# First MLP round of a fused attention, gating and MLP kernel: raw loads queued two slots later, written tiles kept six slots, a tenth tile, deferred VectorE halves, and other orders at the opening and the end

## The chip, the cores and the metric

The kernel runs on one core of a Trainium2 chip. The metric is the device time of one execution in microseconds (us), taken as the median of several runs. The engines are TensorE (PE), VectorE (DVE), ScalarE (ACT), GpSimd (POOL) and SyncE, whose DMA queue is SPq in the trace. Each works through its own instructions in the order in which they were written, and waits for the others on semaphores. All DMAs of this part of the program are issued by SyncE, in one queue.

## The reference

Everything is float32. Sigmoid attention over 4 x 12 heads of 448 rows feeds a gated MLP, and that feeds a channel MLP with a residual:

```python
h = np.maximum(x @ w_in, 0.0)                       # gated MLP
u, v = h[..., :512], h[..., 512:]
v_s = np.einsum('ts,bsd->btd', w_spatial, layernorm(v)) + b_spatial[None, :, None]
x = (u * v_s) @ w_out                               # (4, 448, 768)
xn = (x - mu) / np.sqrt(var + 1e-06) * g_ln         # channel MLP
ch = np.maximum(xn @ w_ch1, 0.0) @ w_ch2            # 768 -> 3072 -> 768
return x + ch
```

The kernel splits each float32 operand into a high part (a cast) and a low part (x minus the cast), and takes each product as three matmuls: high by high, high by low, low by high. The weights arrive as 64-bit floats, which the kernel decodes to float32 with shifts and scalings.

## The kernel before

The program has four stages. Up to some 249 us it computes attention, with the projections of the gated MLP and some weight decoding beside it. From 249 to 284 us it ends the gated MLP's projections and begins the spatial product, and a generator `after_stream` decodes and splits one more set of weights beside them. The spatial product and the output projection last to some 372 us. Then comes the channel MLP, in two rounds of twelve cells: the first on 1024 rows (512 columns a product), from 372 to about 820 us, the second on 768 rows.

One cell takes one of twelve weight groups `g`. Its first product (`w_ch1`) has seven sub-products in Strassen's manner, the P steps, each accumulated in a PSUM bank of its own kind, X or Y; its second product has seven or eight S steps, into the banks `acc`. Steps of neighbouring cells alternate: P 0 of cell i, S 0 of cell i-1, P 1, S 1, and so on. Each step is nine matmuls and is one slot; a cell has fourteen slots, here called s=0 to s=13, with P k at s=2k and S k at s=2k+1 (an eighth S step is behind s=13). Between the steps other work is written out: `settle(t)` is called after each step and issues what `plan` has put at slot `t` of the table `later`, then gives the queued DRAM writes their turn (`tick`), then gives tiles back, then fetches weights.

What lies around the change:

- The evacuation of a P step: `copied` is an ACT copy (L1262), `summed` a DVE add from PSUM (L1266), an ACT relu (L1267) and an ACT cast to the high part (L1251); `low` is the DVE subtraction of the low part (L1257). A later P step that begins a new sum in the bank waits for that evacuation. S3 (the sixth P step, s=10) and A22 (the seventh, s=12) both use X; `add` (L1349) is the DVE addition of an S step's result.
- Weights of groups 2 to 10 (`LATE`) are decoded in the first round. `load` (L353) brings 768 KB of raw words, `scale` is two ACT instructions (L387, L392), `bits` one of DVE (L396). `make` (L807, POOL) forms a sum of two pieces, `split` is an ACT cast (L812) and a subtraction (L813, on POOL for `w_ch1` and on DVE for `w_ch2`) into a tile of 768 columns of `t_all`, and `put` queues the tile's write to DRAM (`wscr`, L902), for the second round.
- Four tiles a cell (T1, T3, T2, T4 of `w_ch2`, at s=6, 7, 8 and 9) are made only for the second round: `staged` writes them out and gives the tile back some slots later. All tiles come from the list `w_free`, first in, first out: eight tiles, and a ninth after the opening.
- A raw buffer's next load is planned in the slot of the `bits` that ends its use. SyncE's queue is in order, so a load that waits for `bits` holds what is behind it.

Of the kernel before, what the change touches and what calls it, by code (L numbers as in the profile page):

```python
# [18 lines left out]
P = 128  # L19
# [51 lines left out]
R_SIZE, T_SIZE, F_SIZE, Q_SIZE = 30976, 6400, 12288, 3072  # L71
# [16 lines left out]
PLACE_W_T = [768 * k for k in range(8)]  # L88
PLACE_OUT = [23552, 24320]
# [24 lines left out]
LAST = [SEVEN[k] for k in (0, 5, 1, 2, 3, 4, 6)]  # L114
# [20 lines left out]
AFTER_JOBS = "d0 d1 - e0 11 e1 21 =T1 22 =T3 T1 =T2 T3 =T4 T2 - T4"  # L135
# [144 lines left out]
def sigmoid_attention_gmlp_mlp(ctx: ExitStack, tc, q, k, v, w_in, w_sp, w_out, g_ln, w1, w2, out):  # L280
# [512 lines left out]
    class Weights:  # L793
# [104 lines left out]
    puts = []  # L898
    put_after = [5]

# [131 lines left out]
    put_after[0] = 1  # L1032

    def after_stream():
        outs = Ring(R, 0, 0)
        outs.blocks = [Block(R, o, 2 * HALF) for o in PLACE_OUT]
        for grp, m in AFTER:
# [4 lines left out]
            for job in AFTER_JOBS.split():  # L1042
                tick()
                weights[grp].do(m, job, outs, nc.scalar.copy)
                yield
        while puts:
# [122 lines left out]
    for j, (u, c) in enumerate(order):  # L1169
# [10 lines left out]
        if j > 11:  # L1180
            proj.turn_parked(order[j - 2][1], banks, nc.vector.tensor_copy)
# [8 lines left out]
        if j == 12:  # L1190
            xn_of(j)
# [6 lines left out]
    X, Y = (ps_1.tile([P, 512], F32, tag="ps1", name="ps1") for _ in range(2))  # L1198
# [3 lines left out]
    w_free = deque(Block(T, o, 2 * HALF) for o in PLACE_W_T)  # L1202
# [13 lines left out]
    class Hidden:  # L1216
# [19 lines left out]
        def product(self, x, name):  # L1236
            ps = acc[0][:, 0] if (self.i, x) == (0, "A12") else {"A12": Y, "S1": Y, "S4": Y}.get(x, X)
# [32 lines left out]
        def s_add(self, name):  # L1270
# [9 lines left out]
            nc.vector.tensor_tensor(self.rt(out), self.rt(a), self.rt(b), op=op)  # L1280
            self.r[name] = self.r.pop(out)
            if name in ("S3", "S4"):
                self.drop({"S3": "H11", "S4": "S2"}[name])
            self.high(name)

        def after(self, x, ps):
# [25 lines left out]
        def step(self, k):  # L1312
            steps = self.steps()
            if k == 0 and self.i and hidden[self.i - 1].seven:
# [3 lines left out]
            for j in range(3):  # L1318
                if self.two:
# [3 lines left out]
                    if (self.i, k) == (2 * NGRP - 1, 6):  # L1323
                        self.add(ps, out, slice(j, j + 1))
                        self.store(out, j)
# [8 lines left out]
            if (self.i, k) == (2 * NGRP - 1, 6):  # L1334
                return
            if out:
                self.add(ps, out)
            if self.i == 2 * NGRP - 1 and k in (1, 4, 5):
                for j in range(3):
                    self.store(steps[k][4], j)  # L1340
# [316 lines left out]
```

## Time and profile before

| | |
|---|---|
| device time, median of 3 runs | 1111.88 us (1111.39 to 1111.99) |
| device time of the profiled execution | 1110.46 us |
| its span in the trace | 1108.6 us |
| PE busy | 1025.7 us (93%) |
| DVE, ACT, POOL busy | 769.9, 502.4, 317.0 us |
| mean granted PE clock | 0.969 |
| DMA | 251.6 MB, mean 227 GB/s |

A busy PE is not PE at its peak: the granted clock tells how fast it runs while busy (1.00 is 2.4 GHz, 0.50 is 1.2 GHz). In the timeline rows a number in square brackets is the engine's idle time before that instruction, and what ended it. Of a busy time with a count behind it (x2), the row covers several instructions in a run.

### The profile page before, as it was taken

The page shows a single profiled execution, that of the slowest core. Times are in us where ns is not written, and L with a number is a line of the kernel's source. Part 1 is how long each engine was busy: PE and PEld are TensorE (multiplying, and loading weights), DVE is VectorE, ACT ScalarE, POOL GpSimd, SP SyncE. Part 2 cuts the span into 40 slices and gives each one's busy share as a digit, 9 for nine tenths or more (in the row PEclk, how much of TensorE's full clock was granted, in tenths as well). Part 3 has the DMA queues.
Part 4 walks back from the last instruction along what each step waited for, and adds up shares of the span by engine and source line. Part 5 has one row for each costly group of instructions (what it writes and reads, how often), then busy time and mean ns, then how long its engine had stood idle before and what let it go on. Part 6 is the DMA issues. An engine that isn't in the chain of part 4 may idle for free.

```text
span 1108.6 us, 14832 instructions
## 1 busy us (share of the span) xinstructions
PE 1025.7 (93%) x5221; PEld 852.6 (77%) x5221; DVE 769.9 (69%) x999; ACT 502.4 (45%) x823; POOL 317.0 (29%) x266
## 2 busy tenths in 40 slices
PE   9999999998999999977977977979799999999996
PEld 5557666687899878755855855858688999999995
DVE  4679888356848678755655646655787779777776
ACT  5765454454646444645445445444432333333331
POOL 3614133023127404634534534532610012000000
PEclk9999999998999999989988988989899999999999
DMA  8857888566224675685575575667599898888884
GB/s 248 264 186 246 294 257 302 185 202 233 83 100 140 215 275 182 219 280 171 181 274 171 191 265 174 207 246 238 183 308 325 252 333 249 249 248 250 249 250 155
DMA packets 95097, 251.59 MB, mean 227 GB/s; under 512 B 12720, under 2 KB 27056, under 8 KB 94896
## 3 DMA queue, kind: packets, MB, share of 16 engines
q1 hardware_dynamic: 89616, 237.23, 64.8%
q0 software_dynamic: 1760, 7.36, 2.1%
q10 hardware_dynamic: 3648, 6.06, 1.6%
q8 instruction: 42, 0.69, 0.3%
q14 instruction: 31, 0.25, 0.1%
HBM read 163.82 MB, written 86.78 MB: 226 GB/s over the span
## 4 chain that ended last, share of the span: by engine, by line
PE 66%; DMA 8%; DVE 8%; issue 7%; POOL 6%; ACT 5%; SPq 0%; POOLq 0%; DVEq 0%; ACTq 0%
PE ps L341 11%; PE ps L342 10%; PE ps L343 10%; DMA wscr<-t_all 7%; PE acc L341 7%; PE acc L342 7%; PE acc L343 7%; PE psa L551 5%; PE ps L511 4%; POOL f_all L807 3%; POOL t_all L813 2%; DVE f_all L1349 1%; PE ps L524 1%; DVE f_all L396 1%; ACT t_all L812 1%
## 5 line engine op out<-in xcount | busy, mean ns | idle before, releaser
L341 PE MATMUL ps<-r_all,t_all 128*128 128x384 f32 (+1 forms) x480 | 182.2, 380 | 61.3 <-DVE f_all L1266 59.5
L1349 DVE TENSOR_TENSOR f_all<-acc,f_all 128x1152 f32<-128x1152 f32 (+2 forms) x135 | 201.5, 1493 | 37.5 <-PE acc L343 37.4
L342 PE MATMUL ps<-r_all,t_all 128*128 128x384 f32 (+1 forms) x480 | 180.4, 376 | 0.0
L343 PE MATMUL ps<-r_all,t_all 128*128 128x384 f32 (+1 forms) x480 | 180.3, 376 | 0.0
L341 PEld LDWEIGHTS ps<-r_all,t_all 128*128 128x128 f32 x480 | 93.3, 194 | 76.8 <-issue 56.4
L813 POOL TENSOR_TENSOR t_all<-f_all,t_all 128x384 fp32r<-128x384 f32 x63 | 69.7, 1106 | 221.8 <-ACT t_all L812 187.7
L1267 ACT ACTIVATE f_all<-f_all 128x512 f32<-128x512 f32 (+1 forms) x72 | 41.7, 579 | 194.9 <-DVE f_all L1266 194.9
L1257 DVE TENSOR_TENSOR r_all<-f_all,r_all 128x384 fp32r<-128x384 f32 (+1 forms) x141 | 105.7, 750 | 30.6 <-ACT r_all L1251 29.4
L813 DVE TENSOR_TENSOR t_all<-f_all,t_all 128x384 fp32r<-128x384 f32 x72 | 49.4, 686 | 108.7 <-ACT t_all L812 93.0
L1251 ACT CAST r_all<-f_all 128x384 fp32r<-128x384 f32 (+1 forms) x141 | 78.5, 557 | 87.7 <-DVE f_all L1280 85.1
L341 PE MATMUL acc<-r_all,t_all 128*128 128x512 f32 x279 | 111.0, 398 | 0.0
L342 PE MATMUL acc<-r_all,t_all 128*128 128x512 f32 x279 | 110.7, 397 | 0.0
L343 PE MATMUL acc<-r_all,t_all 128*128 128x512 f32 x279 | 110.1, 395 | 0.0
L343 PEld LDWEIGHTS ps<-r_all,t_all 128*128 128x128 f32 x480 | 93.6, 195 | 11.3
L342 PEld LDWEIGHTS ps<-r_all,t_all 128*128 128x128 f32 x480 | 93.7, 195 | 10.7
L812 ACT CAST t_all<-f_all 128x384 fp32r<-128x384 f32 x135 | 65.9, 511 | 67.8 <-DMA wscr<-t_all 54.5
L807 POOL TENSOR_TENSOR f_all<-f_all 128x384 f32<-128x384 f32 x72 | 94.0, 1309 | 2.1
L341 PE MATMUL acc<-t_all,r_all 128*128 128x384 f32 x252 | 85.9, 341 | 5.7 <-DVE f_all L1349 2.8
L343 PE MATMUL acc<-t_all,r_all 128*128 128x384 f32 x252 | 85.4, 339 | 0.0
L342 PE MATMUL acc<-t_all,r_all 128*128 128x384 f32 x252 | 84.9, 337 | 0.0
L498 ACT ACTIVATE f_all<-ps,bias_s 128x896 f32<-128x896 f32 x70 | 68.2, 1007 | 34.0 <-PE ps L524 18.9
L341 PE MATMUL ps<-r_all 128*128 128x448 f32 (+1 forms) x201 | 78.3, 390 | 3.8 <-issue 1.6
(195 smaller groups left out, 1993.3 us busy)
## 6 DMA issues: line engine op xcount, KB each, us to landing
t_all<-wscr SPq DMA_DIRECT2D x202, 384.0 KB, 3.8
wscr<-t_all SPq DMA_DIRECT2D x126, 384.0 KB, 6.5
q_all<-in_w SPq DMA_DIRECT2D x42, 768.0 KB, 6.0
wscr<-r_all SPq DMA_DIRECT2D x42, 384.0 KB, 4.2
m_all<-in_v SPq DMA_DIRECT2D x24, 256.0 KB, 3.6
yscr<-f_all SPq DMA_DIRECT2D x14, 384.0 KB, 2.3
f_all<-in_k SPq DMA_DIRECT2D x45, 112.0 KB, 4.1
f_all<-in_q SPq DMA_DIRECT2D x45, 112.0 KB, 3.8
```

Source lines behind the costliest of these rows:

```text
L341: nc.tensor.matmul(ps, lh, rh, start=first, stop=False, skip_group_check=skip)
L342: nc.tensor.matmul(ps, lh, rl, start=False, stop=False, skip_group_check=skip)
L343: nc.tensor.matmul(ps, ll, rh, start=False, stop=last, skip_group_check=skip)
L498: nc.scalar.activation(af, ps[:, :, :S], AF.Sigmoid, bias=bias_s, scale=1.0 / math.sqrt(D))
L511: nc.tensor.matmul(ps[:, j, :S], a[w][rows, kc], a[x][rows], start=(i == 0), stop=(i == 2))
L551: nc.tensor.matmul(a["ps"][rows, :S], a["v"][:, 4 * j + c], af[:, j], start=(p % 2 == 0 and c == 0), stop=(p % 2 == 1 and c == 2),)
L807: eng.tensor_sub(self.f(m, WHERE[m][name]), self.f(m, a), self.f(m, b))
L812: high(t[:, 0], x)
L813: low.tensor_sub(t[:, 1], x, t[:, 0])
L1251: nc.scalar.copy(t[:, 0], self.rt(name))
L1257: (eng or nc.vector).tensor_sub(t[:, 1], self.rt(name), t[:, 0])
L1349: nc.vector.tensor_add(t, x, t)
```

## The change

Loads: a raw buffer's next load is planned two slots behind the `bits` that frees it, not in the same slot; the `bits` of the two `w_ch2` pieces move from s=10 and s=12 to s=11 and s=13, their scales with them, and the splits of `11` and `21` from s=11 and s=13 to s=12 and s=14. Tiles: a staged tile is given back after six slots where it was three, and `w_free` has one more tile, 768 columns of `r_all`. Deferred halves: where a split's subtraction is on DVE, `split` only queues it, and `end_lows` issues it (and then queues the write) at the start of the next `settle`, behind the next step's evacuation. `after_stream` does the same, and its four sums are on DVE where they were on POOL. Banks: X and Y change places in every other cell. Opening: the last normalisations and parked transposes come later, one pair of copies is ACT's, and a low part moves behind the next evacuation. End: the last cell has another order of P and of S steps, two of its sums are on POOL, and its last S step is stored whole.

```diff
-R_SIZE, T_SIZE, F_SIZE, Q_SIZE = 30976, 6400, 12288, 3072
+R_SIZE, T_SIZE, F_SIZE, Q_SIZE = 31232, 6144, 12288, 3072
+PLACE_W_R = 30464
-LAST = [SEVEN[k] for k in (0, 5, 1, 2, 3, 4, 6)]
+LAST = [SEVEN[k] for k in (1, 0, 2, 3, 4, 5, 6)]
+CLOSING = [STEADY[k] for k in (0, 2, 3, 4, 5, 6, 1)]
-AFTER_JOBS = "d0 d1 - e0 11 e1 21 =T1 22 =T3 T1 =T2 T3 =T4 T2 - T4"
+AFTER_JOBS = "d0 d1 - e0 11 e1 21 =T1v 22 =T3v T1 =T2v T3 =T4v T2 - T4"
...
             high(t[:, 0], x)
-            low.tensor_sub(t[:, 1], x, t[:, 0])
-            if name in NAMES:
-                put(wscr[self.g, m, NAMES.index(name)], blk.ap(2 * HALF))
+
+            def end():
+                low.tensor_sub(t[:, 1], x, t[:, 0])
+                if name in NAMES:
+                    put(wscr[self.g, m, NAMES.index(name)], blk.ap(2 * HALF))
+
+            if defer[0] and low is nc.vector:
+                lows.append(end)
+            else:
+                end()
...
-    w_free = deque(Block(T, o, 2 * HALF) for o in PLACE_W_T)
+    w_free = deque([Block(R, PLACE_W_R, 2 * HALF), *(Block(T, o, 2 * HALF) for o in PLACE_W_T)])
...
-            ps = acc[0][:, 0] if (self.i, x) == (0, "A12") else {"A12": Y, "S1": Y, "S4": Y}.get(x, X)
+            ps = acc[0][:, 0] if (self.i, x) == (0, "A12") else XY[(x in ("A12", "S1", "S4")) ^ (self.i & 1)]
...
                 self.low("H12")
-                self.low("H22")
+                if self.i:
+                    self.low("H22")
...
             del weights[g].t[m, name]
-            done.append([put_after[0] + 1, blk])
+            done.append([6, blk])
...
-        for t, m, f in ((-9, 0, 1), (-7, 0, 0), (10, 1, 0), (12, 1, 1)):
+        for t, m, f in ((-9, 0, 1), (-7, 0, 0), (11, 1, 0), (13, 1, 1)):
...
-            first = t
+            first = t + 2
...
-        put_in(t1 - 3, 1, "11", V)
-        put_in(t1 - 1, 1, "21", V)
+        put_in(t1 - 2, 1, "11", V)
+        put_in(t1, 1, "21", V)
...
     def settle(t):
+        end_lows()
         for job in later.pop(t, ()):
             job()
```

DVE, in a cell of the middle of the first round, from s=6 to s=10. Before, the L813 rows are the subtractions of T1, of T3, and of T2 and T4; L1349 is the add of S 3, L396 the `bits` of s=7, and the two L1266 rows are the evacuations of S4 (s=8) and S3 (s=10).

```order
L813 TENSOR_TENSOR t_all<-f_all,t_all 128x384
L1349 TENSOR_TENSOR f_all<-acc,f_all 128x1536
L396 SCALAR_TENSOR_TENSOR f_all<-q_all 128x768
L813 TENSOR_TENSOR t_all<-f_all,t_all 128x384
L1266 TENSOR_TENSOR f_all<-f_all,ps_3298 128x512
L813 TENSOR_TENSOR t_all<-f_all,t_all 128x384 x2
L1266 TENSOR_TENSOR f_all<-f_all,ps_3297 128x512
L1257 TENSOR_TENSOR r_all<-f_all,r_all 128x512 x2
```

The same place of the changed kernel (L817 are the subtractions, L1361 the add, L398 the `bits`, L1280 the evacuations, L1271 the low parts):

```order
L1361 TENSOR_TENSOR f_all<-acc,f_all 128x1536
L817 TENSOR_TENSOR t_all<-f_all,t_all 128x384
L398 SCALAR_TENSOR_TENSOR f_all<-q_all 128x768
L1280 TENSOR_TENSOR f_all<-f_all,ps_3296 128x512
L817 TENSOR_TENSOR t_all<-f_all,t_all 128x384 x2
L1280 TENSOR_TENSOR f_all<-f_all,ps_3295 128x512
L1271 TENSOR_TENSOR r_all<-f_all,r_all 128x512 x2
L817 TENSOR_TENSOR r_all<-f_all,r_all 128x384
```

T1's subtraction now stands behind S 3's add, T3's behind S4's evacuation, and T4's behind the evacuation of S3, where it stood ahead of it.

ACT at the same place, from s=8 on. Before, L1267 and L1251 are the relu and the cast of S4's evacuation, the two L812 the casts for T2 and for the next group's `11`, L387 and L392 a `scale`, and the single L812 the cast for T4:

```order
L1267 ACTIVATE f_all<-f_all 128x512
L1251 CAST r_all<-f_all 128x512
L812 CAST t_all<-f_all 128x384 x2
L387 ACTIVATE q_all<-q_all 128x768
L392 ACTIVATE q_all<-q_all,bias_d 128x768
L812 CAST t_all<-f_all 128x384
```

And in the changed kernel:

```order
L1281 ACTIVATE f_all<-f_all 128x512
L1265 CAST r_all<-f_all 128x512
L814 CAST r_all<-f_all 128x384
L814 CAST t_all<-f_all 128x384 x2
L1281 ACTIVATE f_all<-f_all 128x512
L1265 CAST r_all<-f_all 128x512
L389 ACTIVATE q_all<-q_all 128x768
L394 ACTIVATE q_all<-q_all,bias_d 128x768
```

The three casts now stand together, and the `scale` stands behind the evacuation of S3.

## Rows read from the trace of the kernel before

**Rows 1.** Stages: us, then busy us (instructions) by engine, PE clock, DMA share, GB/s
```profile
249.00:284.00 35.00, 28.31 (x120) 24.17 (x120) 23.24 (x38) 16.98 (x31) 11.19 (x13) 0.90 0.54 187
...
452.00:770.00 318.00, 264.71 (x1075) 211.54 (x1074) 186.57 (x185) 155.51 (x265) 138.84 (x117) 0.92 0.63 215
...
836.00:1088.00 252.00, 250.95 (x1434) 249.16 (x1433) 196.19 (x241) 76.91 (x156) 11.60 (x6) 1.00 0.86 265
1088.00:1108.60 20.60, 11.55 (x58) 9.51 (x57) 13.49 (x17) 1.54 (x3) 0.00 (x0) 0.92 0.34 120
```
**Rows 2.** Waits of PE from 200 us on: total us, times, longest
```profile
PE ps L341 <- DVE f_all L1266: 59.5, 9, 8.0
...
PE acc L341 <- ACT r_all L1251: 2.7, 1, 2.7
...
PE ps L341 <- ACT f_all L1303: 1.9, 2, 1.2
```
**Rows 3.** PE timeline: start, us, instruction, idle before it and its releaser
```profile
482.34 0.76 PE L341 MATMUL ps<-r_all,t_all 128*128 128x512 f32 x1 [7.63 <-DVE f_all L1266]
...
606.27 0.77 PE L341 MATMUL ps<-r_all,t_all 128*128 128x512 f32 x1 [7.74 <-DVE f_all L1266]
606.83 0.63 PE L342 MATMUL ps<-r_all,t_all 128*128 128x512 f32 x1
607.26 0.63 PE L343 MATMUL ps<-r_all,t_all 128*128 128x512 f32 x1
...
610.46 0.39 PE L342 MATMUL acc<-r_all,t_all 128*128 128x512 f32 x1
...
799.96 0.80 PE L341 MATMUL ps<-r_all,t_all 128*128 128x512 f32 x1 [5.76 <-DVE f_all L1266]
...
816.45 0.44 PE L341 MATMUL ps<-r_all,t_all 128*128 128x384 f32 x1 [0.41 <-DVE f_all L1266]
```
**Rows 4.** DVE timeline in one cell of the first round
```profile
591.27 1.36 DVE L813 TENSOR_TENSOR t_all<-f_all,t_all 128x384 fp32r<-128x384 f32 x1
...
594.53 1.75 DVE L396 SCALAR_TENSOR_TENSOR f_all<-q_all 128x768 uint32<-128x768 uint32 x1 [0.22 <-POOL t_all L813]
596.20 0.55 DVE L813 TENSOR_TENSOR t_all<-f_all,t_all 128x384 fp32r<-128x384 f32 x1
596.67 0.67 DVE L1266 TENSOR_TENSOR f_all<-f_all,ps 128x512 f32<-128x512 f32 x1
599.10 0.56 DVE L813 TENSOR_TENSOR t_all<-f_all,t_all 128x384 fp32r<-128x384 f32 x1 [1.76 <-ACT t_all L812]
...
605.44 0.68 DVE L1266 TENSOR_TENSOR f_all<-f_all,ps 128x512 f32<-128x512 f32 x1
```
**Rows 5.** ACT timeline in the same cell
```profile
597.38 0.63 ACT L1267 ACTIVATE f_all<-f_all 128x512 f32<-128x512 f32 x1 [4.61 <-DVE f_all L1266]
...
604.42 0.51 ACT L812 CAST t_all<-f_all 128x384 fp32r<-128x384 f32 x1 [3.26 <-DMA wscr<-t_all]
```
**Rows 6.** POOL timeline in the same cell
```profile
588.09 5.43 POOL L807 TENSOR_TENSOR f_all<-f_all 128x384 f32<-128x384 f32 x4
```
**Rows 7.** Waits of SyncE's queue, 452 to 770 us
```profile
SPq L353 <- DVE f_all L396: 147.0, 28, 9.3
```
**Rows 8.** DMA issues, 452 to 770 us: count, KB each, median us to landing
```profile
wscr<-t_all SPq DMA_DIRECT2D x110, 384.0 KB, 6.7
q_all<-in_w SPq DMA_DIRECT2D x28, 768.0 KB, 6.1
```
**Rows 9.** PE timeline, two shorter stalls and the matmul behind one
```profile
260.92 0.48 PE L343 MATMUL psa<-r_all 128*128 128x448 f32 x1 [2.62 <-DVE r_all L665]
...
374.24 0.47 PE L341 MATMUL ps<-r_all 128*128 128x512 f32 x1 [1.55 <-issue]
374.55 0.40 PE L342 MATMUL ps<-r_all 128*128 128x512 f32 x1
374.78 0.40 PE L343 MATMUL ps<-r_all 128*128 128x512 f32 x1
```

More of the change, by code (lines that the diff above doesn't have):

```diff
@@ L896, in sigmoid_attention_gmlp_mlp, with end_lows @@
     weights = [Weights(g) for g in range(NGRP)]
-    puts = []
+    puts, lows, defer = [], [], [False]
     put_after = [5]
+    def end_lows():
+        while lows:
+            lows.pop(0)()
     def put(dst, src):
@@ L1180, in sigmoid_attention_gmlp_mlp @@
         if j > 11:
-            proj.turn_parked(order[j - 2][1], banks, nc.vector.tensor_copy)
+            proj.turn_parked(order[j - 2][1], banks, nc.vector.tensor_copy if j < 13 else nc.scalar.copy)
         proj.evac(c, ps, y_at[c])
@@ L1197, in sigmoid_attention_gmlp_mlp @@
     acc = [sums_p.tile([P, 3, 512], F32, tag="acc", name="acc") for _ in range(2)]
-    X, Y = (ps_1.tile([P, 512], F32, tag="ps1", name="ps1") for _ in range(2))
+    XY = [ps_1.tile([P, 512], F32, tag="ps1", name="ps1") for _ in range(2)]
     h_free = deque(Block(R, o, 1024) for o in PLACE_H)
     r_free = deque(Block(F, o, 512) for o in PLACE_R)
-    w_free = deque(Block(T, o, 2 * HALF) for o in PLACE_W_T)
+    w_free = deque([Block(R, PLACE_W_R, 2 * HALF), *(Block(T, o, 2 * HALF) for o in PLACE_W_T)])
     dec = [Block(F, o, WC) for o in (F_at["dec"], F_at["dec"] + WC, F_at["xn"], F_at["xn"] + WC)]
@@ L1313, in step @@
             steps = self.steps()
-            if k == 0 and self.i and hidden[self.i - 1].seven:
+            if k == 0 and self.i and hidden[self.i - 1].seven and self.i < 2 * NGRP - 1:
                 swap[0] ^= 1
@@ L1333, in step, with add @@
                 w_free.append(self.w.t.pop((1, wn)))
-            if (self.i, k) == (2 * NGRP - 1, 6):
-                return
             if out:
                 self.add(ps, out)
-            if self.i == 2 * NGRP - 1 and k in (1, 4, 5):
+            if self.i == 2 * NGRP - 1 and not any(t[4] == out for t in rest):
                 for j in range(3):
-                    self.store(steps[k][4], j)
-        def add(self, ps, out, js=slice(0, 3)):
+                    self.store(out, j)
+        def add(self, ps, out):
             u, s = out
             if self.two:
-                t, x = y2[:, js, u, s], ps[:, js, :HALF]
+                t, x = y2[:, :, u, s], ps[:, :, :HALF]
             else:
@@ L1454, in sigmoid_attention_gmlp_mlp @@
                 continue
[L1455 removed]
+            m, name = (0, order_of(c)[k][1]) if kind == "P" else (1, hidden[c].steps()[k][1])
             if (c, m, name) not in seen and (c, m) != (0, 0) and not (c in LATE):
@@ new lines, in sigmoid_attention_gmlp_mlp @@
+    for kind, c, k in (token for seq in tokens for token in seq):
+        if kind == "T":
+            turn_out(k)
+            continue
+        cell, t = hidden[c], clock[kind, c, k]
+        closing = 2 * NGRP - 1
+        if kind == "P":
+            x, name = order_of(c)[k]
+            cell.after(x, cell.product(x, name))
+            if c == 0:
+                if x == "A12":
+                    cell.low("H22")
+                    cell.low("H11")
+                if x == "A22":
+                    cell.low("S1")
+                    w_free.append(w_first["T4"])
+                settle(t)
+                settle(t + 1)
+                continue
+            prev = hidden[c - 1]
+            if k == 0:
+                prev.s_add("S2")
+            elif k in (1, 2, 3):
+                prev.low(("S2", "S4", "S3")[k - 1])
+            elif (c, k) == (NGRP, 6):
+                cell.low("S1")
+            elif (c, k) == (closing, 6):
+                cell.low("H11")
+        else:
+            cell.step(k)
+            cur = hidden[c + 1] if c < closing else None
+            if c == closing:
+                if k == 0:
+                    cell.s_add("S3", G)
+                    cell.low("S4")
+                elif k == 1:
+                    cell.low("S3", G)
+            elif k == 1:
+                cell.s_add("S4")
+            elif k == 2:
+                cell.s_add("S3")
+                cur.low("H11")
+            elif k == 5 and c + 1 == closing:
+                cur.low("S1")
+            elif k == 6:
+                if c + 1 == closing:
+                    cur.s_add("S2")
+                    cur.s_add("S4", low="S2")
+                else:
+                    cur.low("S1" if cur.seven else "H21")
+            if k == 7:
+                continue
+        settle(t)
```

75 lines of the change are left out of this document (14 added, 61 removed).

## Prediction

> **What bounds the kernel now.** First the busy time and the clock by stage [rows 1]: in the second round (836 to 1088 us) PE is busy for 250.95 of 252.00 us at full clock, so nothing that is done there for the other engines can show. Between 452 and 770 us it is busy for 264.71 of 318.00 us, at a mean clock of 0.92; that is where time lies. Then the waits of PE [rows 2]: 59.5 us, in nine waits, are one kind, a P step that waits for the evacuation of its bank (L1266). Then PE's timeline [rows 3]: eight of the nine are long, one in each cell from 482 to 800 us, at the same place of the cell, ahead of P 6 (s=12). The eighth took 5.76 us and the ninth, at 816 us, 0.41 us, so the first seven sum to 59.5 - 5.8 - 0.4 = 53.3 us, 7.6 us each. Behind such a stall the matmuls start 0.43 us apart (606.83, 607.26), where 0.23 us is the pace at full clock (374.55, 374.78) [rows 9]; ten matmuls on, at 610.46, the row is 0.39 us long again and not 0.63. They run at 1.2 GHz first, and ten times 0.20 us are lost. So a cell that stalls loses 7.6 + 2.0 us.
>
> Who holds the evacuation is read on DVE [rows 4]: S3's evacuation at 605.44 stands behind T4's subtraction, and that waited for ACT's cast [rows 5], which began at 604.42 after 3.26 us of waiting for a DRAM write: the tile that it fills was still being written out. The write was late for two reasons. SyncE's queue stood for 147.0 us in this stretch, 28 times, at raw loads that waited for the `bits` of their buffer [rows 7], with finished writes behind them; and once issued, a write lands after 6.7 us at the median [rows 8], while the tile goes back to the list after three slots, of 2.1 us each (nine matmuls at 0.23 us).
>
> **The change, part by part.**
>
> *The seven steady cells.* T4's subtraction moves behind S3's evacuation, T4's cast ahead of the next `scale`, and the tiles that the four casts take have been out of use for longer: T1's goes back at s=11 and is next filled at s=12, some four slots (8.4 us) behind the place of its write in the queue, against 6.7 us to land. T3, T2 and T4 have more. The write is queued a slot later than before, since the subtraction is; that is in the four slots. I take the wait for DRAM as gone.
>
> What is late next is the chain that brings DVE to S3's evacuation. I follow it through the cell shown before. POOL's four sums (588.09, 5.43 us) [rows 6] end at 593.5 and its subtraction for T4 of the other weight a microsecond later; DVE's `bits`, at 594.53, waits for that, as before. Next on DVE now comes S4's evacuation, at 596.20, where T3's subtraction took 0.47 us until 596.67. T2's subtraction waits for ACT's relu and two casts: it began 1.72 us behind the relu (597.38 to 599.10), so it begins at 596.20 + 0.71 + 1.72 = 598.63, and ends 0.47 us later. S3's evacuation then starts at 599.10, and PE 0.83 us behind its start (605.44 to 606.27), at 599.93. PE had run out at 606.27 - 7.74 = 598.53. So 1.4 us of stall are left in a cell. T1's subtraction, moved behind the add of S 3, fills time in which DVE waits for POOL. A stall of 1.55 us left the clock up [rows 9]: the matmuls behind it start 0.23 us apart. Sum: 53.3 - 7 x 1.4 = 43.5 us, and 7 x 2.0 = 14.0 us of slow restarts.
>
> The bounds: no stall left (53.3 us), or 3.0 us left in each (32.3 us), when T3's and T2's subtractions both meet a sum on POOL. DVE's row 591.27, beside POOL's sums, shows such a subtraction at 1.36 us; 596.20, with POOL idle, at 0.55 us. With 3.0 us left the clock may fall again, and the 14.0 us would stay.
>
> The Trainium skill (SBUF — State Buffer, "Who interferes with whom") says that VectorE and GpSimd share one pair of ports as an exclusive lock, which a VectorE instruction with two SBUF inputs takes against a GpSimd instruction that reads SBUF, and the loser waits for the whole of the other. The two durations above agree with it. By that rule alone, with both subtractions hit, the seven cells would keep 1.6 us more each, 11 us in all.
>
> *The raw loads, two slots later.* The time between a load and its `scale` falls from four slots to three for two of the four loads. SyncE issues the nearer one when the `bits` ends (596.3), and ACT now reaches its `scale` at s=12, behind the relu and cast of P 6: 599.93 + 2.1 + 1.2 = 603.2. That leaves 6.9 us, against 6.1 us to landing at the median [rows 8]: no wait, or a short one. What would be late behind it is the cast and subtraction of `11`, wanted by S 0 at s=15; with 0.5 us a cast and 1.7 us of `scale` there are another 2.3 us before PE feels it. Cost nothing; from 9.2 us to landing on, a microsecond each.
>
> *The eighth stall (799.96).* There DVE runs the sums for the second round's input and POOL its splits; ACT's cast and T4's subtraction are only part of the delay. Two subtractions and a wait for ACT leave the path, some 2.6 us of the 5.76. Bounds 0 and 7.8 (with the restart).
>
> *249 to 284 us.* PE is idle for 35.00 - 28.31 = 6.7 us, and the clock of 0.90 costs some 2.8 us more. The first long stall, 2.62 us [rows 9], waits for DVE, which has stood behind subtractions that wait for ACT. Deferring them takes that off, and four sums on DVE (some 0.5 us each) replace POOL sums of 1.3 us that slowed DVE's neighbours. But each split's write is issued one job later with only two tiles, so ACT's wait for the last write, which comes last in the stage, may grow by as much. I take 5 us of the 9.5; bounds -2 and 9.5.
>
> *Opening.* The two waits of 1.9 us in sum for A22's relu [rows 2] go, since the next cell's first P step has the other bank. The other moves there shift a microsecond between ACT and DVE beside an idle engine of the two: nothing. Bounds -1 and 3.
>
> *End.* From 1088 us on PE is busy for 11.55 of 20.60 us [rows 1]. The new order takes the 2.7 us wait [rows 2] apart: S1 no longer shares a bank with the step ahead of it. But S2 follows H11 in one bank at once, so it waits for H11's addition. Storing the last step whole saves three short PE waits and adds two DMA issues behind the last addition. I take 2 us; bounds -1 and 5.
>
> Sum: 43.5 + 14.0 + 2.6 + 5 + 1.9 + 2 = 69.0 us. The profiled execution took 1110.46 us, 1.9 us more than its span; 1110.5 - 69.0 = 1041.5. The median of the runs is 1.4 us above that execution, so 1043 us is the forecast.
>
> **The rivals.**
>
> *DVE and POOL take over the stall.* The 3.0 us of the upper bound remain in each cell, and the clock falls with them: 7 x 1.6 + 14.0 = 25 us less gain, 1068 us. For it: the chain from POOL's sums to S3's evacuation is already later than PE by 1.4 us, and the stall of 2.62 us at 260.92 was followed by slow matmuls. Against it: T3's and T2's subtractions stand where POOL has one instruction left, not four.
>
> *The raw loads land late* (the case on the other side). All of a cell's writes at s=7 to s=10 now share the queue with two loads. If a load needed more than 9.2 us, PE would stall at S 0 of each cell; the kernel would be slower than before from 9.2 + 8.2 = 17.4 us on, since 9.6 - 1.4 = 8.2 us are won in a cell. At 20 us it would cost 2.6 x 7 us more than before, 1120 us with the other gains counted. For it: the loads start later and closer to their use. Against it: 6.1 us at the median, and a DMA share of 0.63 in the stretch; with cells of 33 us instead of 41 the share is 0.79.
>
> The Trainium skill (DMA: Bandwidth & Descriptors, "Queues, rings and completion order") says that a DMA's completion count lands only after every earlier write of the same DMA engine. No row here shows one DMA waiting for another in that way. By it a load behind two writes and another load, 1.6 MB, would be seen some 4.6 us later than its own data, at the 341 GB/s that 215 GB/s at a share of 0.63 come to [rows 1]; that alone would not reach the 9.2 us above.
>
> *A tile is still not written when it is filled.* If T1's write took over 8.4 us in half of the cells, ACT would wait as before, but T4's subtraction no longer stands ahead of S3's evacuation; the relu behind it would be late, and half of the restarts would come back: 1060 to 1075 us.
>
> *No stall is left*, and the stage at 249 us and the end give all that they have: 9.8 + 4.5 + 3 us more, 1026 us.
>
> **How the numbers follow.** The forecast (1034 to 1053 us) has 0.60; DVE and POOL 0.17; no stall left 0.11; tiles 0.06; late loads 0.06, of which half end above the time before. The range, 1024 to 1070 us, holds the first three but for their ends. About 0.2% is what a measurement here can tell from no change. Faster by more than that: 0.95; within it: 0.01; slower: 0.04, nearly all of it late loads.
>
> **What the profile will show.** The wait of PE for the L1280 evacuation falls from 59.5 us to 10 to 15, in single waits of 1 to 2 us ahead of P 6; ACT's casts into tiles show no wait for `wscr`; SyncE's wait at raw loads falls well below 147 us; the clock between 450 and 770 us (which will end some 55 us sooner) is 1.00; raw loads show no wait on ACT over 1 us. The wait of 2.7 us near the end is gone. The prediction is wrong in its main step if waits of over 3 us ahead of P 6 remain, if they come up at S 0, or if the clock still falls once a cell.

## The result and the profile after

The changed kernel takes 1050.97 us (median of 4 runs, 1049.57 to 1051.42) where the one before takes 1111.64: ratio 0.9457, 95% interval 0.944 to 0.9473. The forecast was 1043, with a range of 1024 to 1070. The profiled execution took 1051.18 us, its span is 1049.4 us.

Stages of the changed kernel, as in [rows 1]: us, then busy us (instructions) of PE, PEld, DVE, ACT and POOL, PE clock, DMA share, GB/s.

```profile
249.00:284.00 35.00, 30.02 (x132) 26.11 (x131) 24.57 (x46) 18.33 (x35) 7.19 (x11) 0.90 0.60 195
452.00:776.00 324.00, 308.56 (x1320) 249.85 (x1319) 225.62 (x224) 174.26 (x299) 152.96 (x123) 0.98 0.73 259
776.00:1028.00 252.00, 250.97 (x1434) 248.90 (x1432) 196.12 (x241) 77.10 (x156) 12.60 (x7) 1.00 0.85 263
```

PE now idles for 15 us of the stretch from 452 us on; before it was 53 us [rows 1]. Its waits from 200 us on (total, times, longest):

```profile
PE ps L343 <- DVE f_all L1280: 12.0, 8, 4.2
PE acc L343 <- issue: 4.0, 2, 3.0
PE psa L690 <- DVE r_all L670: 3.6, 1, 3.6
PE acc L343 <- DMA t_all<-wscr: 3.4, 1, 3.4
PE acc L345 <- DVE r_all L817: 1.2, 1, 1.2
```

The first row answers to the 59.5 us of [rows 2] (a line of the program stands 2 to 14 lines further down in this kernel). Its eight waits in the timeline are seven of 1.08 to 1.15 us, one in each of seven cells, and one of 4.23 us; behind that comes a wait for a DMA that the kernel before didn't have:

```profile
601.28 0.47 PE L343 MATMUL ps<-r_all,t_all 128*128 128x512 f32 x1 [1.09 <-DVE f_all L1280]
...
733.77 0.79 PE L343 MATMUL ps<-r_all,t_all 128*128 128x512 f32 x1 [4.23 <-DVE f_all L1280]
734.36 0.63 PE L344 MATMUL ps<-r_all,t_all 128*128 128x512 f32 x1
...
748.10 0.77 PE L343 MATMUL acc<-r_all,t_all 128*128 128x512 f32 x1 [3.39 <-DMA t_all<-wscr]
```

Matched steps of PE show where the 59.2 us of span came from. The marks are the starts of the same matmul in both traces.

| stretch, from and to | before | after | gain | forecast |
|---|---|---|---|---|
| ahead of the stage at 249 us | 249.22 | 250.20 | -1.0 | 0 |
| that stage, to the first 384-wide product | 54.23 | 51.54 | 2.7 | 5 |
| to the first product of the MLP | 66.90 | 66.90 | 0 | 0 |
| opening, to the step ahead of the first long stall | 102.12 | 98.59 | 3.5 | 1.9 |
| seven cells, to the end of the seventh slow restart | 265.00 | 205.78 | 59.2 | 57.5 |
| eighth and the rest of the round, to the first run of matmuls on the tile `warm` (1.47 us) | 96.20 | 100.38 | -4.2 | 2.6 |
| second round, to its last change of bank | 251.68 | 251.33 | 0.4 | 0 |
| end | 23.25 | 24.68 | -1.4 | 2 |

Where the 1.1 us come from is read on DVE, in the cell that ends with the stall at 601.28:

```profile
594.15 0.80 DVE L817 TENSOR_TENSOR t_all<-f_all,t_all 128x384 fp32r<-128x384 f32 x1
595.86 1.75 DVE L398 SCALAR_TENSOR_TENSOR f_all<-q_all 128x768 uint32<-128x768 uint32 x1 [0.91 <-POOL t_all L817]
597.53 0.68 DVE L1280 TENSOR_TENSOR f_all<-f_all,ps 128x512 f32<-128x512 f32 x1
598.13 0.55 DVE L817 TENSOR_TENSOR t_all<-f_all,t_all 128x384 fp32r<-128x384 f32 x1
599.98 0.56 DVE L817 TENSOR_TENSOR t_all<-f_all,t_all 128x384 fp32r<-128x384 f32 x1 [1.30 <-ACT t_all L814]
600.45 0.68 DVE L1280 TENSOR_TENSOR f_all<-f_all,ps 128x512 f32<-128x512 f32 x1
```

The order is the one that the prediction followed: `bits`, S4's evacuation, T3's subtraction, T2's behind ACT's relu and casts, S3's evacuation. None of ScalarE's casts into tiles waits for a write to DRAM. SyncE's wait at raw loads fell from 147.0 us [rows 7] to 26.7, and a write that took 6.7 us to land [rows 8] now takes 2.9 (waits of SyncE's queue, and DMA issues, 425 to 752 us). The queue as a whole did not stand much less: its wait for GpSimd's subtractions into `t_all`, whose writes come next, went from 54.2 us (452 to 770 us) to 149.4.

```profile
SPq L355 <- DVE f_all L398: 26.7, 25, 2.0
```
```profile
wscr<-t_all SPq DMA_DIRECT2D x108, 384.0 KB, 2.9
```

### The profile page after: what moved, and what is told of

Read it like the earlier page. It is cut to its first block, busy times and chain, and to the rows that moved or that the text cites. A ratio compares the mean times of both kernels' runs of the same rounds, so it can differ in the third digit from the quotient of the medians.

```text
span 1049.4 us, 14789 instructions
## 1 busy us (share of the span) xinstructions
PE 1013.9 (97%) x5221; PEld 846.1 (81%) x5221; DVE 761.1 (73%) x997; ACT 500.7 (48%) x825; POOL 307.6 (29%) x264
## 4 chain that ended last, share of the span: by engine, by line
PE 70%; issue 10%; DVE 6%; POOL 6%; DMA 3%; ACT 3%; SPq 0%; ACTq 0%; POOLq 0%; DVEq 0%
PE ps L343 12%; PE ps L345 11%; PE ps L344 11%; PE acc L343 7%; PE acc L345 7%; PE acc L344 7%; PE psa L553 6%; PE ps L513 5%; POOL f_all L809 3%; POOL t_all L817 2%; PE ps L526 1%; DVE f_all L1361 1%; DVE f_all L1280 1%; ACT t_all L814 1%; DVE t_all L817 1%
## 5 line engine op out<-in xcount | busy, mean ns | idle before, releaser
L1361 DVE TENSOR_TENSOR f_all<-acc,f_all 128x1152 f32<-128x1152 f32 (+1 forms) x133 | 201.4, 1514 | 56.6 <-PE acc L345 56.5
L343 PE MATMUL ps<-r_all,t_all 128*128 128x384 f32 (+1 forms) x426 | 157.0, 369 | 12.0 <-DVE f_all L1280 12.0
L345 PE MATMUL ps<-r_all,t_all 128*128 128x384 f32 (+1 forms) x426 | 156.3, 367 | 0.0
L344 PE MATMUL ps<-r_all,t_all 128*128 128x384 f32 (+1 forms) x426 | 156.1, 366 | 0.0
L1271 DVE TENSOR_TENSOR r_all<-f_all,r_all 128x384 fp32r<-128x384 f32 (+1 forms) x140 | 100.7, 720 | 27.3 <-ACT r_all L1265 26.1
L817 POOL TENSOR_TENSOR t_all<-f_all,t_all 128x384 fp32r<-128x384 f32 x57 | 66.6, 1168 | 150.3 <-ACT t_all L814 147.8
L343 PE MATMUL acc<-r_all,t_all 128*128 128x512 f32 x246 | 98.4, 400 | 3.4 <-DMA t_all<-wscr 3.4
L343 PEld LDWEIGHTS ps<-r_all,t_all 128*128 128x128 f32 x426 | 80.5, 189 | 24.3 <-ACT t_all L814 9.1
L343 PE MATMUL ps<-r_all 128*128 128x512 f32 (+2 forms) x255 | 97.7, 383 | 0.7 <-DVE f_all L693 0.7
L344 PE MATMUL acc<-r_all,t_all 128*128 128x512 f32 x246 | 98.3, 400 | 0.0
L345 PE MATMUL acc<-r_all,t_all 128*128 128x512 f32 x246 | 98.0, 398 | 0.0
L344 PE MATMUL ps<-r_all 128*128 128x512 f32 (+2 forms) x255 | 96.2, 377 | 0.0
L345 PE MATMUL ps<-r_all 128*128 128x512 f32 (+2 forms) x255 | 96.1, 377 | 0.0
L345 PEld LDWEIGHTS ps<-r_all,t_all 128*128 128x128 f32 x426 | 80.5, 189 | 9.2
L344 PEld LDWEIGHTS ps<-r_all,t_all 128*128 128x128 f32 x426 | 80.6, 189 | 8.9
L809 POOL TENSOR_TENSOR f_all<-f_all 128x384 f32<-128x384 f32 x72 | 85.4, 1191 | 2.6 <-DVE t_all L817 0.6
L500 ACT ACTIVATE f_all<-ps,bias_s 128x896 f32<-128x896 f32 x70 | 68.2, 1006 | 34.7 <-PE ps L526 18.4
L343 PE MATMUL acc<-t_all,r_all 128*128 128x384 f32 x225 | 77.1, 343 | 4.2 <-issue 4.0
L345 PE MATMUL acc<-t_all,r_all 128*128 128x384 f32 x225 | 76.7, 341 | 0.0
L344 PE MATMUL acc<-t_all,r_all 128*128 128x384 f32 x225 | 76.4, 339 | 0.0
```

Of the source, the lines that this page charges most:

```text
L343: nc.tensor.matmul(ps, lh, rh, start=first, stop=False, skip_group_check=skip)
L344: nc.tensor.matmul(ps, lh, rl, start=False, stop=False, skip_group_check=skip)
L345: nc.tensor.matmul(ps, ll, rh, start=False, stop=last, skip_group_check=skip)
L500: nc.scalar.activation(af, ps[:, :, :S], AF.Sigmoid, bias=bias_s, scale=1.0 / math.sqrt(D))
L809: eng.tensor_sub(self.f(m, WHERE[m][name]), self.f(m, a), self.f(m, b))
L1271: (eng or nc.vector).tensor_sub(t[:, 1], self.rt(name), t[:, 0])
```

## The experiments

### Which part took the stall away

Three parts of the change act on the seven cells: later raw loads, longer rest for the tiles, and deferred subtractions. The theory was that the rest of the tiles decides. Three kernels take one part back from the changed kernel.

**u_loads**: `- first = t + 2`, `+ first = t`.

> The changed kernel with the raw loads queued where they were before: in the slot of the bits that free their buffer, not two slots later. Theory (the tiles' rest decides: a tile now lies six slots before it is filled again, so a write that starts 2 us later still lands in time): SyncE waits at raw loads again, over 100 us in the first round, and still the stall ahead of P 6 stays near 1.1 us a cell; 1051 to 1056 us. Rival (the queue decides: writes held behind waiting loads are what made the casts late): casts wait for DRAM writes again, stalls of 4 us or more in each of seven cells with slow restarts behind them, 1080 us or more.

1050.65 us (ratio to before 0.946, 0.9444 to 0.9475). SyncE stands at raw loads for 129.0 us again (its waits, 425 to 752 us, below), and writes land after 7.2 us at the median. The stall stays at 1.1 us, as PE's timeline shows:

```profile
SPq L355 <- DVE f_all L398: 129.0, 32, 7.1
```
```profile
601.95 0.47 PE L343 MATMUL ps<-r_all,t_all 128*128 128x512 f32 x1 [1.11 <-DVE f_all L1280]
```

**u_keep**: `- done.append([6, blk])`, `+ done.append([put_after[0] + 1, blk])`, and `w_free` without the tenth tile.

> The changed kernel with the tiles of the DRAM writes given back after three slots again and without the tenth tile. Theory (the tile's rest decides): ScalarE's casts wait for DRAM writes again, the relu behind them is late, and stalls of 3 us or more ahead of P 6, with slow restarts, come back in most cells: 1075 to 1110 us. Rival (the deferred subtraction decides, since S3's evacuation no longer stands behind a subtraction that waits for the cast): casts may wait, but PE does not, 1051 to 1058 us.

1050.13 us (0.9455, 0.9441 to 0.9469). No cost here either, against the theory. But the rival's reason doesn't hold by this alone: casts wait for writes only 3.0 us in all, in two waits outside the seven cells (447.50 and 694.76), and writes land after 2.9 us.

```profile
600.62 0.47 PE L343 MATMUL ps<-r_all,t_all 128*128 128x512 f32 x1 [1.08 <-DVE f_all L1280]
```

**u_defer**: `put_after[0], defer[0] = 2, False` where the first round begins.

> The changed kernel with VectorE's subtractions of the first round issued right behind their cast again, not a slot later. Theory (the tile's rest decides): the casts wait for no write, so T4's subtraction only adds itself (0.5 us) and half a microsecond of waiting for its cast ahead of S3's evacuation: stall of about 2.1 us instead of 1.1 in each of seven cells, 1056 to 1062 us, up to 1074 if the clock falls behind the longer stall. Rival (the deferral is what took the stall away): stalls of 5 us or more, 1090 us or more.

1076.28 us (0.9689, 0.9668 to 0.9709). Between the two forecasts: stalls of 3.17 to 3.28 us, 2.1 more than with deferral and 1.1 more than I had taken, and slow restarts behind most of them. On DVE, T2's and T4's subtractions both stand ahead of S3's evacuation, and each waits for its cast:

```profile
613.79 0.56 DVE L817 TENSOR_TENSOR t_all<-f_all,t_all 128x384 fp32r<-128x384 f32 x1 [1.76 <-ACT t_all L814]
614.62 1.04 DVE L817 TENSOR_TENSOR t_all<-f_all,t_all 128x384 fp32r<-128x384 f32 x1 [0.27 <-ACT t_all L814]
615.58 0.67 DVE L1280 TENSOR_TENSOR f_all<-f_all,ps 128x512 f32<-128x512 f32 x1
```

So neither the loads nor the rest costs anything to take back, and the deferral costs 25 us. That looks as if the deferral were all of it. Three kernels add one part alone to the kernel before.

**b_loads1**: `first = t + 2` alone.

> The kernel before with one part of the change alone: each raw load of the first round is queued two slots later. Theory (u_loads and u_keep cost nothing because later loads and longer rest each end the casts' wait for DRAM writes, and that wait is worth the step from 7.6 us of stall to the 3.2 us of u_defer): SyncE's 147 us at raw loads are mostly gone, casts wait for no write, stalls of 3.2 to 4 us in seven cells: 1072 to 1084 us. Rival (the wait for the write never mattered by itself, the subtraction ahead of S3's evacuation did): stalls stay above 6 us, 1095 to 1111 us.

1088.81 us (0.9796, 0.9776 to 0.9817): above the theory's 1084. The casts wait for no write, and stalls of 4.3 us stay, not 3.2: ACT still runs a `scale` (588.76, 589.55) ahead of T4's cast, which the changed kernel has behind it.

```profile
588.76 0.89 ACT L387 ACTIVATE q_all<-q_all 128x768 f32<-128x768 f32 x1
589.55 0.97 ACT L392 ACTIVATE q_all<-q_all,bias_d 128x768 uint32<-128x768 uint16 x1
590.41 0.51 ACT L812 CAST t_all<-f_all 128x384 fp32r<-128x384 f32 x1
```
```profile
592.25 0.47 PE L341 MATMUL ps<-r_all,t_all 128*128 128x512 f32 x1 [4.33 <-DVE f_all L1266]
```

**b_keep**: the tenth tile, and `done.append([5, blk])`.

> The kernel before with another part alone: a tenth tile, and a tile rests five slots behind its write is split, not three (six don't fit without the later casts of 11 and 21). Theory: SyncE still waits at raw loads for 100 us or more, but the casts wait for no write or under 1 us a cell, stalls of 3.2 to 4.5 us: 1072 to 1088 us. Rival (the write wait never mattered by itself): stalls above 6 us, 1095 to 1111 us.

1087.29 us (0.9785, 0.9767 to 0.9803), in the theory's range. SyncE waits 126.4 us at raw loads, the casts for no write; stalls of 4.3 to 4.5 us.

```profile
593.14 0.47 PE L342 MATMUL ps<-r_all,t_all 128*128 128x512 f32 x1 [4.47 <-DVE f_all L1267]
```

**b_defer**: `end` and `end_lows` as in the changed kernel, switched on in the first round only.

> The kernel before with the third part alone: VectorE's subtractions of the first round come one slot later. Theory (two causes in one chain, each with its own share): the casts still wait for writes by about 3 us a cell, and as ScalarE runs in order the relu of the product ahead of S3 or the cast for T2's subtraction is late by part of that; stalls of 2 to 5 us, 1062 to 1090 us. Rival (the deferral is sufficient, because T4's cast is the only one that waits and nothing urgent stands behind it any more): stalls near 1.1 us, 1051 to 1060 us.

1112.41 us (1.0011, 0.9995 to 1.0027): no gain at all, and outside both forecasts. The stall ahead of P 6 is down to 1.1 us, and a new one of 5.66 us stands one product further on, with slow matmuls behind it:

```profile
597.63 0.47 PE L341 MATMUL ps<-r_all,t_all 128*128 128x512 f32 x1 [1.09 <-DVE f_all L1277]
...
609.80 0.80 PE L341 MATMUL ps<-r_all,t_all 128*128 128x512 f32 x1 [5.66 <-ACT f_all L1314]
```

ACT shows why: T4's cast waits 4.90 us for the write, and behind it, in order, come the relu of S3's sum (603.72), a `scale`, a cast that waits another 1.65 us for something that the trace does not name, and then A22's relu (609.16), which empties the bank that the next cell's first product needs. Without the other parts the deferral only hands the wait for the write to the next step.

```profile
603.30 0.51 ACT L812 CAST t_all<-f_all 128x384 fp32r<-128x384 f32 x1 [4.90 <-DMA wscr<-t_all]
...
609.16 0.59 ACT L1314 ACTIVATE f_all<-ps 128x512 f32<-128x512 f32 x1
```

Together (medians; the kernel before had 1110 to 1112 in these comparisons):

| | none | loads | rest | both |
|---|---|---|---|---|
| subtractions at once | 1111 | 1089 | 1087 | 1076 |
| deferred | 1112 | 1050 | 1051 | 1051 |

(Upper row: before, b_loads1, b_keep, u_defer; lower: b_defer, u_keep, u_loads, the changed kernel.) The column "both" and the lower cells of "loads" and "rest" also hold the changed kernel's other edits: the cast ahead of the `scale` (about 1.1 us a cell, if all of the difference between b_loads1's stalls of 4.3 us and u_defer's of 3.2 is put down to it; it wasn't tried alone), the stage at 249 us and the opening. Two waits stand in one chain. Either of loads and rest ends the wait for the write; the deferral takes T4's subtraction, and its wait for the cast, out of the way of S3's evacuation. One without the other leaves a stall; later loads and longer rest do the same thing twice.

### The 1.1 us that were left

**x_two**: every deferred subtraction of the first round waits two slots.

> The changed kernel with VectorE's subtractions of the first round two slots later instead of one, so that T2's no longer stands ahead of S3's evacuation and waits there for ScalarE's cast (1.30 us in the changed kernel's trace). Theory (this wait is the stall of 1.1 us that is left): the stalls ahead of P 6 go, 7 us less: 1042 to 1046 us. Rival (the stall comes from S4's evacuation being late behind the bits and GpSimd's four sums, and ScalarE's relu behind it sets the pace): stalls of 0.8 us or more stay, 1049 to 1052 us.

1069.65 us (0.9629, 0.9609 to 0.9649). In the eighth cell one subtraction of T4 reads data that A12's load has replaced, so this version computes a wrong result; the seven cells are not touched by that. Both forecasts missed. The stalls ahead of P 6 are gone, but `11`, `21`, `12` and `22` are used directly from their tiles, and now their low halves are late for the S steps, 2.1 and 0.85 us in a cell:

```profile
590.44 0.50 PE L345 MATMUL acc<-r_all,t_all 128*128 128x512 f32 x1 [2.08 <-DVE t_all L817]
```

**x_t2**: only T2's subtraction is later (the number counts slots), and A12 is loaded through GpSimd.

```diff
-lows.append(end)
+lows.append([2 if late[0] and (m, name) == (1, "T2") else 1, end])
...
-plan(t + 10, lambda: x_load("A12"))
-plan(t + 11, lambda: x_split("S3", "A21"))
+plan(t + 11, lambda: x_split("S3", "A21"), lambda: x_load("A12", G))
```

> The changed kernel with two edits that lie in different stretches. First, of the deferred subtractions only T2's comes another slot later, behind S3's evacuation. Theory: the 1.1 us left ahead of P 6 in seven cells is S3's evacuation behind T2's subtraction, which waits 1.30 us for ScalarE; the stalls go, 7.8 us. Rival: the evacuation of S4 and ScalarE's relu behind it, late from GpSimd's four sums, set the pace; stalls of 0.8 us or more stay. Second, the load of the second round's A12 is issued by GpSimd behind its split of S3, not by SyncE. Theory: the new stall of 3.39 us at 748 us is a fetch that stood in SyncE's queue behind this load, which waited 8.7 us for a deferred subtraction; it goes, with 0 to 2 us of slow clock behind it. Rival: the fetch is late because its tile comes free late; the stall stays over 2 us. Both theories: 1038 to 1041 us; first alone 1042 to 1044; second alone 1045 to 1048; neither 1050 to 1052.

1042.96 us (0.9385, 0.9365 to 0.9404). The first edit did what the theory said: no PE wait of 0.2 us or more stands in the seven cells, for S3's evacuation comes 1.07 us behind the start of S4's:

```profile
591.19 0.67 DVE L1282 TENSOR_TENSOR f_all<-f_all,ps 128x512 f32<-128x512 f32 x1
591.79 0.55 DVE L817 TENSOR_TENSOR t_all<-f_all,t_all 128x384 fp32r<-128x384 f32 x1
592.26 0.68 DVE L1282 TENSOR_TENSOR f_all<-f_all,ps 128x512 f32<-128x512 f32 x1
```

The second edit missed. The fetch that had stood behind the load is in time, but the load now lands after 5.9 us at the median, not 2.9, and ACT's cast of A12 waits for it with PE behind. Whether GpSimd as its issuer made it slower isn't shown: nine fetches of 384 KB, which the changed kernel issued only behind the load (from 743.33 on), were issued here (731.50 to 736.08) before it had landed.

```profile
739.14 1.15 ACT L1398 CAST r_all<-f_all 128x1152 fp32r<-128x1152 f32 x1 [5.93 <-DMA f_all<-xscr]
```
```profile
740.35 0.69 PE L343 MATMUL ps<-r_all 128*128 128x384 f32 x1 [5.78 <-ACT r_all L1398]
```

### The eighth cell and the end

In the changed kernel's eighth cell DVE's add at 717.33 ran beside GpSimd's split, and so did the next ones; S4's evacuation came at 730.12, after PE had run out (729.54). The kernel before has the same: its add took 3.86 us, and S4's evacuation came at 794.58, PE having run out at 794.20. Before, then the changed kernel:

```profile
781.75 3.86 DVE L1388 TENSOR_TENSOR q_all<-q_all 128x1152 f32<-128x1152 f32 x1 [1.60 <-POOL r_all L1385]
```
```profile
717.33 3.84 DVE L1400 TENSOR_TENSOR q_all<-q_all 128x1152 f32<-128x1152 f32 x1
...
730.12 0.68 DVE L1280 TENSOR_TENSOR f_all<-f_all,ps 128x512 f32<-128x512 f32 x1
```

**u_close_v**: `x_split(name, x, eng=nc.vector)` instead of GpSimd, and the last cell's order and stores as before.

> The changed kernel with two edits that lie in different stretches. First, the order of the last cell and its stores as before. Theory: the new order lost 1.4 us from 1025 us on, as the two traces differ there (23.3 us before, 24.7 us after); undone, the end is 1.4 us shorter. Rival: the loss lies in something else of the end (the final stores by chance): no change. Second, in the eighth cell all splits of the second round's input are on VectorE and none on GpSimd. Theory: the stall of 4.23 us ahead of P 6 there is VectorE held up beside GpSimd's splits (its add took 3.84 us at 717.33, and 1.35 us with GpSimd idle); without them the stall falls to 0 to 2.5 us. Rival: VectorE has no room for five more splits of 1.35 us, and the stall stays at 4 us or grows. Both theories: 1045 to 1048 us; first alone 1049 to 1051; neither 1051 to 1054.

1045.18 us (0.9394, 0.9372 to 0.9415). From the cell's first product (704.33 in the changed kernel) to the run of `warm` matmuls at 776.83 took 72.50 us; here 65.84, 6.7 less. The same add takes 1.35 us. But the stall ahead of P 6 is still 3.40 us, more than forecast: the split of S2 stands ahead of S3's evacuation and waits for ACT. So the theory's stall gave only 0.8 of the 6.7 us. What went is the wait of 3.39 us for the fetch (T4's subtraction ends at 736.0, not at 740.3, and A12's load is issued at 736.08, not at 740.37), and 3.4 us of slow matmuls behind the stalls (PE busy 61.07 us instead of 64.49); two short waits, 0.29 and 0.67 us, came in.

```profile
718.27 1.35 DVE L1405 TENSOR_TENSOR q_all<-q_all 128x1152 f32<-128x1152 f32 x1
...
731.54 1.36 DVE L1402 TENSOR_TENSOR r_all<-f_all,r_all 128x1152 fp32r<-128x1152 f32 x1 [0.91 <-ACT r_all L1401]
732.82 0.68 DVE L1280 TENSOR_TENSOR f_all<-f_all,ps 128x512 f32<-128x512 f32 x1
```

The end didn't get shorter. From the third run of `warm` matmuls (840.45 before, 780.17 in the changed kernel) to the end of the span it took 268.1 to 269.8 us in five profiles with the old order, and 267.6 to 269.3 us in nine with the new one. The order at the end is worth nothing that these profiles can tell.

**u_s5xy**: the stage at 249 us and the banks undone (`AFTER_JOBS` without its v's, `defer` from the first round on, `XY[x in ("A12", "S1", "S4")]`).

> The changed kernel with two smaller parts undone, which lie in different stretches of the trace: in the stage at 249 to 284 us the subtractions follow their casts at once and all sums are on GpSimd again; and the first products of every cell use the same PSUM bank again. Theory: the stage costs 2.7 us more, as the two traces differ there, and the opening 1.9 us more (the waits for A22's relu come back): 1054 to 1057 us. Rival (the gain of those stretches came from elsewhere, from the moved subtractions of the opening or from later raw loads): within 1 us of the changed kernel, 1050 to 1052 us.

1054.64 us (0.9491, 0.9472 to 0.951): 3.7 us more, in the theory's range, though the two kernels' intervals just touch. The profiled execution was the shortest of the four, 1050.91. The stage takes 54.54 us in it, 3.0 more than in the changed kernel; the bank's share, from the MLP's first product to the eighth cell, is 336.54 against 335.69 us, 0.9 where 1.9 was expected. It is no longer as a whole because it spent 1.4 us less ahead of the stage and 2.4 less in the eighth cell, where the matmuls behind a wait of 3.51 us for the same fetch stayed at full clock.

### The version that beats both

**best_v**: T2's later subtraction and all splits on VectorE; everything else is the changed kernel.

> The changed kernel with the two edits that gained: T2's subtraction behind S3's evacuation (the seven stalls of 1.1 us were gone in x_t2), and all splits of the second round's input on VectorE (6.6 us less between 704 and 777 us in u_close_v); the load of A12 stays with SyncE. Theory: both gains are in different stretches and add up: 1051.0 - 7.8 - 6.6 = 1036.6 us, 1035 to 1039. Rival: x_t2 lost time in the eighth cell because T2's later subtraction, not the load on GpSimd, kept ScalarE waiting 5.93 us; then a stall of 4 us or more comes back at the step behind P 6 there, 1039 to 1044 us.

1036.75 us (0.9327, 0.9313 to 0.9341), where the sum of the two gains was 1036.6. That it fits so closely is in part luck: in the traces the seven cells gave 9.5 us (205.78 to 196.25), not 7.8, and the eighth 5.2 (72.50 to 67.30), not 6.6, since a wait of 1.46 us for a fetch came back. ScalarE's long wait didn't come back: it went with the load's move to GpSimd, not with T2's subtraction.

**best_vg**: S2's split back on GpSimd.

> The same, but the split of S2 stays on GpSimd: on VectorE it stands ahead of S3's evacuation and waits 0.91 us for ScalarE there (731.54 in u_close_v). Theory: S3's evacuation comes 1.4 us or more sooner, the stall ahead of P 6 in the eighth cell is below 1.5 us, and the kernel 1 to 3 us below best_v: 1034 to 1037 us. Rival: GpSimd's split then holds up VectorE's work behind it, as in the changed kernel, and what is won is given back: within 1 us of best_v.

1034.88 us (0.9317, 0.9301 to 0.9333). The interval overlaps best_v's, so the two can't be told apart by time. The trace says where the rest went: the stall ahead of P 6 is down from 3.40 to 0.56 us, and PE then waits 3.78 us for a fetch, where best_v waits 1.46.

```profile
732.41 0.48 PE L343 MATMUL acc<-r_all,t_all 128*128 128x512 f32 x1 [3.78 <-DMA t_all<-wscr]
```

## Why the prediction was right, step by step

- *The seven cells* were right in mechanism and size: 59.2 us for 57.5. The 1.4 us left per cell measured 1.1, by the chain that was worked out; x_t2 removed it by moving the one subtraction in it. The 14 us of slow restarts went too: behind a stall of 1.1 us the first row is 0.47 us long. What the prediction didn't say is that later loads and longer rest are two cures for one wait, and that the deferral alone is worth nothing. Of its signs, the casts without a wait came, and so did the clock in these cells (1.00). But one wait of over 3 us ahead of P 6, which it named as a sign that its main step is wrong, remains in the eighth cell (4.23 us), and the clock falls there: that is the eighth stall, below.
- *Raw loads at no cost*: right. They land after 4.8 us at the median, 6.9 were there, and no ACT wait for them shows. The rival that they come late is out.
- *The eighth stall* is the step that failed: "Two subtractions and a wait for ACT leave the path, some 2.6 us", bounded by 0 from below. The stretch became 4.2 us longer. Between the evacuations of S4 and S3 DVE had T2's subtraction, which waited for ACT, an add, and T4's subtraction. Now it has T3's subtraction, the same add, and T2's. So one subtraction came in for the one that left; only the wait of 1.76 us went, and PE's stall shrank by 1.5 us, from 5.76 to 4.23. Before:

```profile
794.58 0.68 DVE L1266 TENSOR_TENSOR f_all<-f_all,ps 128x512 f32<-128x512 f32 x1
797.01 0.56 DVE L813 TENSOR_TENSOR t_all<-f_all,t_all 128x384 fp32r<-128x384 f32 x1 [1.76 <-ACT t_all L812]
797.49 1.35 DVE L1388 TENSOR_TENSOR f_all<-q_all,f_all 128x1152 f32<-128x1152 f32 x1
798.75 0.55 DVE L813 TENSOR_TENSOR t_all<-f_all,t_all 128x384 fp32r<-128x384 f32 x1
799.22 0.68 DVE L1266 TENSOR_TENSOR f_all<-f_all,ps 128x512 f32<-128x512 f32 x1
```

And behind S4's evacuation at 730.12 in the changed kernel, with T4's subtraction as the last row:

```profile
730.72 0.55 DVE L817 TENSOR_TENSOR t_all<-f_all,t_all 128x384 fp32r<-128x384 f32 x1
731.19 1.35 DVE L1400 TENSOR_TENSOR f_all<-q_all,f_all 128x1152 f32<-128x1152 f32 x1
732.56 0.56 DVE L817 TENSOR_TENSOR t_all<-f_all,t_all 128x384 fp32r<-128x384 f32 x1
733.03 0.68 DVE L1280 TENSOR_TENSOR f_all<-f_all,ps 128x512 f32<-128x512 f32 x1
...
737.31 3.00 DVE L817 TENSOR_TENSOR t_all<-f_all,t_all 128x384 fp32r<-128x384 f32 x1
```

Against that gain stand the new wait of 3.39 us for the fetch and 2.8 us more of slow matmuls (PE is busy for 92.76 us of the stretch, before 89.99), less a wait of 0.41 us at 816.45 that went. What was left out is A12's load. It goes to the buffer that the last T4 is subtracted from. Deferred, that subtraction stood behind S3's evacuation and two low parts and took 3.00 us beside GpSimd's splits. So the load waited 8.7 us in SyncE's queue, where it had waited 0.86. The fetch that PE missed, issued ahead of the load before (797.97, the load 799.34), now came behind it (742.43, the load 740.37). That this made the fetch late is borne out by u_keep, which issued its fetch ahead of the load (733.30), by x_t2, where the load left SyncE's queue, and by u_close_v, where the subtraction ended 4.3 us sooner: PE waits at most 0.31 us for that fetch in any of them. The deferral moved a step past a queue, and that queue should have been followed. GpSimd's splits hold up VectorE in both kernels (adds of 3.86 and 3.84 us), so they don't explain by themselves why the stretch became longer. From the eighth cell's first product to the second run of `warm` matmuls, the four kernels without deferral in it take 68.2 to 68.3 us, and the seven with it (and with GpSimd's splits) 69.0 to 74.8. The wait in the queue (8.7 us, once, 715 to 752 us):

```profile
SPq L1392 <- DVE t_all L817: 8.7, 1, 8.7
```

- *249 to 284 us*: 2.7 us where 5 were taken, inside the bounds. The counter-effect that was named came: ACT's wait for the two tiles' writes went from 3.8 to 5.3 us, and the two first stalls (2.62 and 1.41 us) became 0.50 and 3.64 us. The sums on VectorE and the deferral weren't tried apart.
- *Opening*: 3.5 us for 1.9. The waits for the relu went, and the wait of 1.55 us at 374.24 [rows 9] too, to which the prediction gave nothing; a new one of 1.16 us came at 446.72, a subtraction deferred past its use (without the deferral, in u_defer, this stretch takes 97.14 us, not 98.59). Which of the moved copies did it wasn't tried; the banks alone account for 0.9.
- *End*: nothing for 2. The 2.7 us wait of [rows 2] went, and a wait of 2.96 us came ahead of S2, at the place that the prediction named. Its row names no releaser; DVE's addition of 1032.40, which took 1.34 us, ends 0.1 us ahead of it:

```profile
1033.85 0.66 PE L343 MATMUL acc<-t_all,r_all 128*128 128x384 f32 x1 [2.96 <-issue]
```

Of the 9.8 us between the forecast sum of 69.0 and the 59.2 measured, the eighth cell makes 6.8, the end 3.4, and the stage at 249 us 2.3; another 1.0 was lost ahead of it, where nothing is changed; the opening and the seven cells gave 3.3 more than taken, the second round 0.4.

## What to carry to other kernels

When a stall has two waits in one chain, take both away before judging either: here deferring alone gained nothing, ending the wait for the write alone gained 22 to 24 us, and both, with the smaller parts of the change, 60. Then look at what the deferred work holds: the buffer that it still reads, the load into that buffer, and the queue behind that load. And where two remedies cure one wait, a test that takes one back shows no cost for either, and doesn't say that the wait was harmless.

## What the runs showed of the hardware

- A 384 KB write landed after 2.8 to 2.9 us at the median where raw loads were queued two slots later (changed kernel, u_keep, b_loads1), and after 7.1 to 7.2 us where they weren't (u_loads, b_keep), with the same bytes in a cell. The Trainium skill (DMA: Bandwidth & Descriptors, "Queues, rings and completion order") says that a completion lands only after every earlier write of the same DMA engine; a write behind a load of 768 KB would land late by that rule too, but no run here separates the order of completion from plain sharing of bandwidth.
- An add of two 128x1152 operands on VectorE took 1.35 us with no split of GpSimd beside it (u_close_v), and 3.84 us beside a split and the sum behind it (changed kernel); T4's 128x384 subtraction took 0.55 and 3.00 us in the same two traces.
- Stalls of one length didn't always cost the clock: in u_defer a cell behind 3.28 us of stall ran at a mean granted clock of 0.95, the next, behind 3.21 us, at 1.00, the one behind 3.23 us at 0.94. The matmuls behind the first one ran at full clock for two rows before they slowed, 0.43 us apart.
